# Retention and a SwiGLU block on one core: gate multiplies placed later, bank reads issued before retention steps, a third place for chunks

## The chip, the cores and the metric

The kernel runs on one core of a Trainium2 chip. Its time is device time in microseconds (us), the median of several runs. TensorE (PE) does matmuls into eight banks of PSUM; VectorE (DVE), ScalarE (ACT) and GpSimd (POOL) work on data in SBUF, the first two also read the banks; SyncE (SP) issues most of the DMA transfers, in order, from one queue. Each engine executes its own instructions in the order in which the program issued them. "PEld" is the loading of weights into PE, which overlaps the matmuls.

## The reference

```
state = gamma * state + k_t v_t^T          (per batch and head, for each t of 768)
y_t   = q_t state / sqrt(64)               -> x (3072 x 512): batch, time | head, dim
out   = (silu(x w_gate) * (x w_val)) w_out (512 -> 1536 -> 512)
```

Four batches, eight heads of 64, float32 throughout.

## The kernel before

Time is cut in chunks of 128 (six for each batch), and the work in four segments: a segment holds three chunks of each of two batches, so six chunks in all. The retention part of a chunk consists of `scores` (q and k against each other, masked by VectorE), `mix` (the output, copied to `xT` by ScalarE) and `state` (the running state). `retention(s)` returns these as a list of small steps, 24 with the sums behind them, and they are woven into other work.

All large products are done by Strassen's method in Winograd's form: 2 x 2 blocks, seven products in place of eight, with sums of blocks before and after. For segment 0, `up` computes gate and value block by block while the weights arrive. From segment 1 on, `up2` uses two nested levels, so the weights come as 21 units of seven blocks (three groups of four feature blocks, seven products each), in a ring of six slots, `ring[0]` to `ring[5]`. Where a unit's sums have not been made yet, `load_unit` fetches four blocks of seven from `unit_b`, `sums_u` makes the other three on VectorE in three steps (the last one also issues the store to `unit_t`). Later the whole unit is read from `unit_t`. Half of the units are summed during `down` of segment 0, the others in `up2` of segment 1.

`up2(s, prepared, at_end)` writes down the order by hand: each of its 21 stages registers events with a time, counted in products (stage n begins at 7 n; its seven products stand at +0, +2, ... +12, so two stages interleave), and the events are issued sorted by time. A product goes into bank `x`, `wb` or `z`; the next product into the same bank adds to it, so it waits until the last result has been read (events at +0.5, +2.5, ... +12.5, by ScalarE's copy or VectorE's add). GpSimd adds the blocks on the diagonal that ScalarE has copied (`pool`, +2.6). For product 3 of a group (`p == 3`), VectorE then multiplies the finished half `h0` with the gate in `p1` (line 564), in two blocks; for product 4 it does the same for `h1` (line 567).

`down(s, u, step)`, for three row blocks u, is the last product: seven products of six steps of k each (line 607), after four sums `sum_h` on VectorE (line 596; for u = 0 they stand ahead of `down`, later ones inside). After each product its helper calls `step`, 21 times for a segment, and `step` issues retention steps of the next segment (`retain`) and then, in segment 0, loads and sums of units; in later segments loads of the first units for the next `up2`. The two first products, `first(0)` and `first(1)`, need no sums.

A chunk is four tiles (`kt`, `qt`, `vn`, `kn`, 256 KB each). Two places for chunks lie in `loadp`. Two chunks are loaded ahead: in segment 0 after `up`, otherwise at the end of `up2`, as `loadp` comes free. Each further chunk is loaded by `last(n)` when the chunk two before it is done. GpSimd multiplies `kn` and `qt` by decays (lines 320 and 323) as soon as they are there.

Of the kernel before, what the change touches and what calls it, by code (L numbers as in the profile page):

```python
# [41 lines left out]
def tile_retnet_swiglu(  # L42
# [72 lines left out]

    def places_of(n):

        return [loadp[:, ts(4 * (n % 2) + i, 512)] for i in range(4)]

    def seg_chunks(s):  # L120

# [26 lines left out]
                          in_=wt[f].rearrange("p a (k f) -> p a k f", k=KH))  # L148

    units = {}  # L150
    ring_turn = [0]

    def load_unit(n, whole):
        t = ring[ring_turn[0] % RING].rearrange("p (h a b) -> p h a b", h=2, a=7)
        ring_turn[0] += 1
        if whole:
            nc.sync.dma_start(out=t, in_=unit_t[n])
        else:
            nc.sync.dma_start(out=t[:, :, ds(U11, 4)],
                              in_=unit_b[n // 7][:, SLOT[PRODUCTS[n % 7]]])  # L160
        units[n] = t
# [202 lines left out]
    def retention(s):  # L364

        cs = seg_chunks(s)

        def last(n):  # L370
            state(cs[n])
            del chunks[cs[n]]
            if s and n + 2 < len(cs):
                load_chunk(cs[n + 2], places_of(n))

        steps = [lambda: scores(cs[0])]
        for n, c in enumerate(cs):
# [106 lines left out]
    def up2(s, prepared, at_end):  # L484
# [23 lines left out]
        def stage(n):  # L508
            q, i = divmod(n, 7)
            base, odd, p = 7 * n, n % 2, PRODUCTS[i]  # L510
            halves = lambda b: banks[b][:, :TH].rearrange("p (h t) -> p h t", h=2)
            x = halves(((4, 0), (5, 1))[odd][n // 2 % 2])
            wb, z = halves(2 + odd), halves(6 + odd)
            h0, h1 = (hT[:, ds(4 * q, 4), i] for i in range(2))
            old, c = {1: (None, p1), 5: (None, p5), 6: (p1, u2), 2: (p1, p1),
                      7: (u2, u2), 3: (h0, h0), 4: (u2, u2)}[p]
            t = hsp[:, ds((2 + odd) * 4 * HT, 4 * HT)].rearrange(
                "p (m h t) -> p m h t", m=2, h=2)
            a = x1[p].rearrange("p k (h t) -> p k h t", h=2)
            sums = op2[p].rearrange("p (m t) -> p m t", m=4)  # L520

            def product(o, slot, rhs, start):
                w = units[n]
                for h in range(2):
                    nc.tensor.matmul(o[:, h], w[:, h, slot], rhs,  # L525
                                     start=(start and h == 0), stop=True,
                                     skip_group_check=True)
# [24 lines left out]

            def by_block(t1, t0, fn):

                for b, when in ((1, t1), (0, t0)):
                    at(base + when, fn, ds(2 * b, 2))

            if p in (6, 7):
                to = h0 if p == 6 else h1
                by_block(9.5, 13.5, lambda r: pool(to[:, r], u2[:, r], p5[:, r], op=add))  # L560
            elif p == 2:
                by_block(10.2, 14.2, lambda r: silu(p1[:, r]))
            elif p == 3:
                by_block(10.7, 13.7, lambda r: tt(h0[:, r], h0[:, r], p1[:, r], op=mul))  # L564
# [18 lines left out]
    def a_dn(i, j, u):  # L583
        return hT[:, ds(FH * j, FH), i, ts(u, P)]
# [11 lines left out]
        nc.vector.tensor_tensor(t, a, b, op=op)  # L596
        hs[n] = t

    first_dn = {}

    def down(s, u, step):
        x = banks[u % 2][:, :DH]
        cur = dict(hs)

        def product(o, slot, a, start=True):
            for k in range(FH):
                nc.tensor.matmul(o, a[:, k], wot[k][:, slot], start=(start and k == 0),  # L607
                                 stop=(k == FH - 1), skip_group_check=True)
            step()

        def tmp(i):
            return iop[:, ts(8 + i, DH)]

        def first(u):
            o = banks[u % 2][:, :DH]
            product(o, B11, a_dn(0, 0, u))
            first_dn[u] = tmp(u % 2)
            nc.scalar.copy(first_dn[u], o)

        def more(*ns):  # L620
            for n in ns:
                if u + 1 < L:
                    sum_h(n, u + 1)

        ev = [iop[:, ts(2 * (u % 2) + i, DM)] for i in range(2)]
        tt = nc.vector.tensor_tensor
        if u not in first_dn:
            first(u)
        if u == 0:
            first(1)  # L630
        p1 = first_dn.pop(u)
        wb = bank("wz")[:, :DH]
        product(wb, T1, cur[1])
        p5 = tmp(2)
        nc.scalar.copy(p5, wb)
        product(x, T2, cur[2], start=False)
        u2 = tmp(3)
        nc.scalar.copy(u2, x)
        product(wb, B22, cur[4], start=False)
        tt(ev[0][:, DH:], wb, u2, op=ALU.add)  # L640
        more(1, 2, 4)
        product(x, T3, cur[3], start=False)
        tt(ev[1][:, DH:], x, p5, op=ALU.add)  # L643
        more(3)
        z = bank("wz")[:, :DH]
        product(z, B21, a_dn(0, 1, u))
        tt(ev[0][:, :DH], z, p1, op=ALU.add)
        product(x, T4, a_dn(1, 1, u), start=False)
        nc.scalar.copy(ev[1][:, :DH], x)
        p, pos = divmod(s * L, NCK)  # L650
        for i in range(2):
            row = (2 * p + i) * S + (pos + u) * P
            nc.scalar.dma_start(out=out[ds(row, P)], in_=ev[i])


    def table(nm):
# [67 lines left out]
        late.pop(0)()  # L724


    resident = list(range(RING))
    to_sum = list(range(RING + 1, NU, 2)) + resident
    prepared = set(to_sum)

    for s in range(NSEG):
        nxt = seg_chunks(s + 1) if s + 1 < NSEG else []
        if s == 0:
            for i in range(2):
                load_chunk(nxt[i], places_of(i))
            ring_turn[0] = 4
        else:

            up2(s, prepared, [(7 * (NU - 5 + 2 * i) + 13.4,
                               lambda i=i: load_chunk(nxt[i], places_of(i)))  # L740
                              for i in range(2)] if nxt else [])
            prepared = set(range(NU))
        for n in (1, 2, 4, 3):
            sum_h(n, 0)
# [6 lines left out]
        def step():  # L751

            k = count[0] = count[0] + 1
            retain(1 + (k % 2 and 2 < k < 14))
            if not nxt:
                return
            if s:
                if k > 7 and k % 2 == 0 and k // 2 - 4 < RING:
                    load_unit(k // 2 - 4, True)
                return  # L760
            if count[1] < len(to_sum) and count[1] * 20 < (k + 2) * len(to_sum):
                load_unit(to_sum[count[1]], False)
                sums.extend(sums_u(to_sum[count[1]]))
                count[1] += 1
            while sums and count[2] * 20 < (k - 1) * 3 * len(to_sum):
                sums.pop(0)()
# [58 lines left out]
```

## Time and profile before

| | us |
|---|---|
| median of 3 runs | 788.09 |
| lowest and highest run | 785.54, 789.98 |
| the profiled execution's own time | 788.89 |
| its span, first to last instruction | 786.8 |
| first product of `down` in segment 0 | at 172.82 |
| `up2` of segments 1, 2, 3: first product to first product of `down` | 101.4, 101.9, 101.9 |
| `down` of segments 0, 1, 2: first product to first product of `up2` | 87.5, 79.5, 83.4 |

A line of the timeline gives the start, how long it lasts, the engine, the line of the program, the operation with its tiles and shapes and, in square brackets, how long the engine had been idle and what released it. A line of the waits gives the waiting engine and line, who released it, the us in total, the number of times and the longest one. A line of a window gives the busy time of PE, PEld, DVE, ACT and POOL in it, the clock granted to PE (1.00 is full speed), the share of the DMA engines that was busy and the GB/s. A product of `up2` is four matmul records (x4), one of `down` twelve.

### The profile page before, as it was taken

To read this page: it belongs to the slowest core of one execution; us is meant where nothing else is said; L and a number is where in the kernel's file an instruction comes from. 1 tells how busy PE (TensorE), PEld (TensorE's weight loads), DVE (VectorE), ACT (ScalarE), POOL (GpSimd) and SP (SyncE) were. 2 spreads that over 40 slices of the span, in tenths; PEclk is the share of its full clock that TensorE was granted. 3 is DMA by queue.
4 is the path that set the end of the run, shared out by engine and by line. 5 is a ranking of instruction groups with operands and counts; after the bars stand their busy time and mean duration, and the time that the engine had idled before them with its cause. 6 is when DMAs were issued, how large, how long until landed. Compare 5 with 4: busy or idle time off the path is not lost.

```text
span 786.8 us, 10948 instructions
## 1 busy us (share of the span) xinstructions
PE 731.1 (93%) x4196; PEld 630.0 (80%) x4196; DVE 493.5 (63%) x782; ACT 224.7 (29%) x440; POOL 288.9 (37%) x183
## 2 busy tenths in 40 slices
PE   5788889889799999999999999998999999998998
PEld 4655445558688989997888999997788899998886
DVE  2788888885758487877445366658265357567520
ACT  2464445411111324331212223331121133332100
POOL 3666666723110173554220072546120043727000
PEclk9999999999999999999999999999999999999999
DMA  9966676454789466752364255551157145640010
GB/s 318 304 194 213 210 246 212 164 186 173 269 293 360 162 207 233 258 204 89 104 241 178 74 189 186 188 174 41 61 174 281 47 150 187 215 152 1 1 53 28
DMA packets 60675, 138.08 MB, mean 175 GB/s; under 512 B 4560, under 2 KB 27600, under 8 KB 60624
## 3 DMA queue, kind: packets, MB, share of 16 engines
q1 hardware_dynamic: 57168, 131.09, 48.6%
q10 hardware_dynamic: 3456, 6.29, 2.3%
q8 instruction: 33, 0.54, 0.3%
q14 instruction: 18, 0.15, 0.1%
HBM read 100.80 MB, written 36.57 MB: 175 GB/s over the span
## 4 chain that ended last, share of the span: by engine, by line
PE 62%; DVE 11%; issue 3%; ACT 1%; DMA 1%; POOL 0%; ACTq 0%; SPq 0%; DVEq 0%
PE bank L525 30%; PE bank L607 23%; DVE hsp L596 3%; PE bank L359 2%; PE bank L308 2%; PE bank L355 2%; DVE iop L490 2%; PE bank L337 1%; PE bank L413 1%; DVE hT L564 1%; DMA loadp<-in_q_t_dram 1%; DVE hT L490 1%; DVE midp L314 1%; ACT midp L490 1%; DVE ring L169 1%
## 5 line engine op out<-in xcount | busy, mean ns | idle before, releaser
L525 PE MATMUL bank<-loadp,ring 128*128 128x192 f32 x720 | 141.0, 327 | 2.2 <-ACT midp L490 2.2
L607 PE MATMUL bank<-wot,hsp 128*128 128x256 f32 x576 | 132.2, 385 | 0.0
L525 PEld LDWEIGHTS bank<-loadp,ring 128*128 128x128 f32 x720 | 120.4, 190 | 4.9 <-ACT midp L490 4.9
L607 PEld LDWEIGHTS bank<-wot,hsp 128*128 128x128 f32 x576 | 108.7, 192 | 15.9 <-issue 0.7
L490 DVE TENSOR_TENSOR iop<-bank,iop 128x384 f32<-128x384 f32 x144 | 79.4, 553 | 61.3 <-PE bank L525 59.3
L607 PE MATMUL bank<-wot,hT 128*128 128x256 f32 x432 | 98.7, 382 | 2.7 <-DVE iop L643 2.7
L607 PEld LDWEIGHTS bank<-wot,hT 128*128 128x128 f32 x432 | 80.9, 190 | 15.3 <-DVE iop L643 3.2
L525 PE MATMUL bank<-xs,ring 128*128 128x192 f32 x432 | 87.9, 326 | 0.0
L490 POOL TENSOR_TENSOR iop<-hsp,midp 128x768 f32<-128x768 f32 x9 | 16.3, 1812 | 193.5 <-ACT hsp L490 193.5
L560 POOL TENSOR_TENSOR hT<-iop 128x768 f32<-128x768 f32 x36 | 66.5, 1847 | 35.8 <-DVE iop L490 35.8
L525 PEld LDWEIGHTS bank<-xs,ring 128*128 128x128 f32 x432 | 73.2, 190 | 0.0
L490 ACT COPY hsp<-bank 128x384 f32<-128x384 f32 x90 | 42.9, 479 | 99.5 <-PE bank L525 88.8
L525 PE MATMUL bank<-xT,ring 128*128 128x192 f32 x324 | 66.2, 327 | 2.3 <-DVE iop L490 2.3
L413 PE MATMUL bank<-xT,ring 128*128 128x384 f32 x144 | 54.6, 526 | 13.5 <-DVE hT L436 13.5
L413 PE MATMUL bank<-xs,ring 128*128 128x384 f32 x192 | 64.8, 488 | 1.8 <-DVE xs L397 1.0
L525 PE MATMUL bank<-hsp,ring 128*128 128x192 f32 x288 | 58.2, 330 | 8.1 <-DVE iop L490 8.1
L413 PEld LDWEIGHTS bank<-xs,ring 128*128 128x128 f32 x192 | 36.3, 191 | 28.9 <-ACT iop L432 1.9
L413 PEld LDWEIGHTS bank<-xT,ring 128*128 128x128 f32 x144 | 29.0, 205 | 36.2 <-issue 20.1
L525 PEld LDWEIGHTS bank<-xT,ring 128*128 128x128 f32 x324 | 54.8, 190 | 3.4 <-DVE iop L490 3.2
L525 PEld LDWEIGHTS bank<-hsp,ring 128*128 128x128 f32 x288 | 47.9, 190 | 11.2 <-DVE iop L490 10.5
L490 DVE TENSOR_TENSOR midp<-bank,midp 128x384 f32<-128x384 f32 x72 | 40.0, 555 | 26.1 <-PE bank L525 24.5
L362 ACT COPY xT<-bank 128x512 f32<-128x512 f32 x24 | 14.1, 587 | 146.8 <-PE bank L359 146.8
(120 smaller groups left out, 985.3 us busy)
## 6 DMA issues: line engine op xcount, KB each, us to landing
ring<-unitt SPq DMA_DIRECT2D x49, 896.0 KB, 4.6
unitt<-ring SPq DMA_DIRECT2D x21, 896.0 KB, 4.6
unitb<-ring SPq DMA_DIRECT2D x12, 896.0 KB, 4.9
ring<-unitb SPq DMA_DIRECT2D x21, 512.0 KB, 6.1
out_dram<-iop ACTq DMA_DIRECT2D x24, 256.0 KB, 2.3
loadp<-in_w_out_dram SPq DMA_DIRECT2D x20, 256.0 KB, 4.3
loadp<-in_k_t_dram SPq DMA_DIRECT2D x18, 256.0 KB, 4.8
loadp<-in_q_t_dram SPq DMA_DIRECT2D x18, 256.0 KB, 4.6
```

What stands on the lines that cost most here:

```text
L169: sub(w[:, :, U1 : U3 + 1 : 3], w[:, :, ds(U3, 2)], w[:, :, U11 : U3 + 1 : 2], op=ALU.subtract)
L308: nc.tensor.matmul(sp[i][:, ts(n, P)], kt[r, n], qt[r, n], start=True, stop=True, skip_group_check=True)
L314: nc.vector.tensor_tensor(t, pairs(sp[i]), mask[:, i], op=ALU.mult)
L355: nc.tensor.matmul(y[:, ts(n, P)], prev[:, n], qd[:, n], start=(n == 0), stop=False, skip_group_check=True)
L359: nc.tensor.matmul(y[ds(D * i, D), ts(n, P)], vn[:, ts(2 * n + i, D)], a[i][:, n], start=(ci == 0 and n == 0), stop=True, skip_group_check ...
L362: nc.scalar.copy(xT[:, :, c // NCK % 2, ts(ci % L, P)], pairs(y))
L413: nc.tensor.matmul(o, w[:, slot, k], a[:, k], start=(start and k == 0), stop=(stop and k == KH - 1), skip_group_check=True)
L490: events.append((t, len(events), lambda: fn(*args, **kw)))
L525: nc.tensor.matmul(o[:, h], w[:, h, slot], rhs, start=(start and h == 0), stop=True, skip_group_check=True)
L560: by_block(9.5, 13.5, lambda r: pool(to[:, r], u2[:, r], p5[:, r], op=add))
L596: nc.vector.tensor_tensor(t, a, b, op=op)
L607: nc.tensor.matmul(o, a[:, k], wot[k][:, slot], start=(start and k == 0), stop=(k == FH - 1), skip_group_check=True)
```

## The change

Four things. (1) The two multiplies of product 3's gate move from +10.7 and +13.7 to +15.8 and +14.3 (and change places). (2) In `down`, `step()` is called after the bank read that follows a product, not inside `product`; `retain` issues nothing at the first two calls, one retention step at the third and fourth, two at the fifth to twelfth, then one. (3) A third place for chunks lies in `ring[4]` and `ring[5]`. Three chunks are loaded ahead, and a further one when the chunk three before it is done. So during `down` the units use only four ring slots: twelve units instead of thirteen are summed in segment 0 (units 5, 7, ... 19 and 0 to 3), one more in `up2` of segment 1 (unit 4), and units 4 and 5 are loaded at the head of `up2`. (4) Two of the six steps of `first(0)` are issued inside the last stage of `up2`, ahead of its last product (`begin`).

```diff
     def places_of(n):
-        return [loadp[:, ts(4 * (n % 2) + i, 512)] for i in range(4)]
+        if n % 3 == 2:
+            return [ring[4 + i // 3][:, ts(i % 3, 512)] for i in range(4)]
+        return [loadp[:, ts(4 * (n % 3) + i, 512)] for i in range(4)]
...
-    def load_unit(n, whole):
-        t = ring[ring_turn[0] % RING].rearrange("p (h a b) -> p h a b", h=2, a=7)
-        ring_turn[0] += 1
+    def load_unit(n, whole, slot=None):
+        t = ring[n % RING if slot is None else slot]
+        t = t.rearrange("p (h a b) -> p h a b", h=2, a=7)
...
-            if s and n + 2 < len(cs):
-                load_chunk(cs[n + 2], places_of(n))
+            if s and n + 3 < len(cs):
+                load_chunk(cs[n + 3], places_of(n))
...
             elif p == 3:
-                by_block(10.7, 13.7, lambda r: tt(h0[:, r], h0[:, r], p1[:, r], op=mul))
+                by_block(15.8, 14.3, lambda r: tt(h0[:, r], h0[:, r], p1[:, r], op=mul))
...
     def down(s, u, step):
...
         def product(o, slot, a, start=True):
             for k in range(FH):
                 nc.tensor.matmul(o, a[:, k], wot[k][:, slot], start=(start and k == 0),
                                  stop=(k == FH - 1), skip_group_check=True)
-            step()
...
-        def first(u):
+        def first(u, ks=range(FH)):
             o = banks[u % 2][:, :DH]
-            product(o, B11, a_dn(0, 0, u))
-            first_dn[u] = tmp(u % 2)
-            nc.scalar.copy(first_dn[u], o)
+            for k in ks:
+                nc.tensor.matmul(o, a_dn(0, 0, u)[:, k], wot[k][:, B11], start=(k == 0),
+                                 stop=(k == FH - 1), skip_group_check=True)
+            if FH - 1 in ks:
+                first_dn[u] = tmp(u % 2)
+                nc.scalar.copy(first_dn[u], o)
+                step()
...
+        if u is None:
+            return first
...
-        if u not in first_dn:
+        if u == 0:
+            first(0, range(begun[0], FH))
+            first(1)
+        elif u not in first_dn:
             first(u)
-        if u == 0:
-            first(1)
...
         nc.scalar.copy(p5, wb)
+        step()
         product(x, T2, cur[2], start=False)
...
-    resident = list(range(RING))
-    to_sum = list(range(RING + 1, NU, 2)) + resident
+    resident = list(range(RING - 2))
+    to_sum = list(range(RING - 1, NU, 2)) + resident
...
-            for i in range(2):
+            for i in range(3):
                 load_chunk(nxt[i], places_of(i))
...
+            ends = [(7 * n + 13.4, lambda i=i: load_chunk(nxt[i], places_of(i)))
+                    for i, n in ((0, NU - 5), (2, NU - 4), (1, NU - 3)) if nxt]
+            def begin(s=s):
+                begun[0] = 2
+                down(s, None, None)(0, range(2))
+            ends.append((7 * (NU - 1) + 11, begin))
+            for n in range(RING - 2, RING):
+                ends.append((-1, lambda n=n: load_unit(n, n in prepared)))
+            up2(s, prepared, ends)
...
-            retain(1 + (k % 2 and 2 < k < 14))
+            retain((k > 2) + (4 < k < 13))
...
-                if k > 7 and k % 2 == 0 and k // 2 - 4 < RING:
+                if k > 7 and k % 2 == 0 and k // 2 - 4 < RING - 2:
                     load_unit(k // 2 - 4, True)
...
-                load_unit(to_sum[count[1]], False)
-                sums.extend(sums_u(to_sum[count[1]]))
+                n = to_sum[count[1]]
+                load_unit(n, False, n if n in resident else count[1] % (RING - 2))
+                sums.extend(sums_u(n))
```

More of the change, by code (lines that the diff above doesn't have):

```diff
@@ L150, in tile_retnet_swiglu @@
     units = {}
-    ring_turn = [0]
-    def load_unit(n, whole):
-        t = ring[ring_turn[0] % RING].rearrange("p (h a b) -> p h a b", h=2, a=7)
-        ring_turn[0] += 1
+    def load_unit(n, whole, slot=None):
+        t = ring[n % RING if slot is None else slot]
+        t = t.rearrange("p (h a b) -> p h a b", h=2, a=7)
         if whole:
@@ L597, in sum_h @@
         hs[n] = t
-    first_dn = {}
+    first_dn, begun = {}, [0]
     def down(s, u, step):
-        x = banks[u % 2][:, :DH]
+        x = banks[(u or 0) % 2][:, :DH]
         cur = dict(hs)
@@ L638, in down @@
         nc.scalar.copy(u2, x)
+        step()
         product(wb, B22, cur[4], start=False)
@@ L641, in down @@
         more(1, 2, 4)
+        step()
         product(x, T3, cur[3], start=False)
@@ L644, in down @@
         more(3)
+        step()
         z = bank("wz")[:, :DH]
@@ L647, in down @@
         tt(ev[0][:, :DH], z, p1, op=ALU.add)
+        step()
         product(x, T4, a_dn(1, 1, u), start=False)
@@ L653, in down @@
             nc.scalar.dma_start(out=out[ds(row, P)], in_=ev[i])
+        step()
     def table(nm):
@@ L733, in tile_retnet_swiglu @@
         if s == 0:
-            for i in range(2):
+            for i in range(3):
                 load_chunk(nxt[i], places_of(i))
-            ring_turn[0] = 4
         else:
-            up2(s, prepared, [(7 * (NU - 5 + 2 * i) + 13.4,
-                               lambda i=i: load_chunk(nxt[i], places_of(i)))
-                              for i in range(2)] if nxt else [])
+            ends = [(7 * n + 13.4, lambda i=i: load_chunk(nxt[i], places_of(i)))
[7 more added lines that the diff above has]
+            up2(s, prepared, ends)
             prepared = set(range(NU))
```

## The prediction

> **What bounds the kernel now.** I read the profile's page first, then the waits of TensorE (PE), then its timeline stage by stage.
>
> ```profile
> span 786.8 us, 10948 instructions
> ...
> PE 731.1 (93%) x4196; PEld 630.0 (80%) x4196; DVE 493.5 (63%) x782; ACT 224.7 (29%) x440; POOL 288.9 (37%) x183
> ```
>
> PE is busy for 731.1 of 786.8 us, so this kernel is a chain of matmuls with holes, and the most that a reordering can win is the 55.7 us of holes. Part of them lies in the load phase and in the first feed-forward pass, which the change doesn't touch. I therefore look for holes where it does: in the three `up2` passes and the four `down` passes. I write up2(1) for `up2` of segment 1, and so on.
>
> ```profile
> PE bank L525 <- DVE iop L490: 10.4, 10, 1.5
> ...
> PE bank L525 <- ACT midp L490: 2.2, 9, 0.5
> ```
>
> The columns are us in total, times, longest. In `up2` (line 525) PE waits 12.6 us in 19 places, always for a bank to be read. One of these places, in up2(2), the whole timeline around it, PE's matmuls with the other engines between:
>
> ```profile
> 468.97 0.81 PE L525 MATMUL bank<-xs,ring 128*128 128x192 f32 x4
> ...
> 469.82 0.56 DVE L490 TENSOR_TENSOR hT<-bank,hT 128x384 f32<-128x384 f32 x1 [0.67 <-PE bank L525]
> ...
> 470.11 1.81 POOL L490 TENSOR_TENSOR iop<-hsp,iop 128x768 f32<-128x768 f32 x1
> 470.29 2.45 DVE L564 TENSOR_TENSOR hT<-hT,midp 128x768 f32<-128x768 f32 x1
> ...
> 471.57 0.81 PE L525 MATMUL bank<-xT,ring 128*128 128x192 f32 x4
> ...
> 473.26 0.92 PE L525 MATMUL bank<-hsp,ring 128*128 128x192 f32 x4 [0.88 <-DVE iop L490]
> ...
> 474.06 0.94 DVE L564 TENSOR_TENSOR hT<-hT,midp 128x768 f32<-128x768 f32 x1
> ...
> 475.64 0.92 PE L525 MATMUL bank<-loadp,ring 128*128 128x192 f32 x4 [0.16 <-ACT midp L490]
> ```
>
> Here is the heart of the case. At 470.11 GpSimd starts a sum that lasts 1.81 us. At 470.29 VectorE starts a gate multiply of line 564 on data in SBUF; it takes 2.45 us, ending 0.8 us after GpSimd's sum, while the same multiply at 474.06, with GpSimd silent, takes 0.94 us. Everything behind it on VectorE is late, among it the read of a bank that PE needs at 472.22 and gets at 473.26. The multiply at 474.06 then delays ScalarE's copy into `midp`, and PE waits again until 475.64. From 468.97 to 471.57 lie four products, 0.65 us each; from 468.97 to 475.64 there should be eight, 5.20 us, and there are 6.67. One boundary between two groups of four blocks thus costs 1.47 us.
>
> **The change part by part: the gate multiplies.** The events of `up2` are sorted by time in products. The two multiplies go from 10.7 and 13.7 to 15.8 and 14.3: both behind the bank reads at 11.5, 12.5 and 13.5, one also behind that at 15.5. Nothing is added or removed. I work it through at the place above. A bank is read 0.85 us after its product's start (468.97, then 469.82) for about 0.55 us. The reads at 11.5, 12.5, 13.5 then start at 470.47, 471.12 and 471.77, the last ends at 472.33, and GpSimd ended at 471.92. So the first multiply runs free, 472.33 to 473.27. ScalarE's copy, which has to wait for it, ends at 473.8 if it takes as long as a bank read; PE needs it at 468.97 + 8 x 0.65 = 474.17. The read at 15.5 follows until 473.8, the second multiply until 474.8, the copy behind it until 475.3; PE needs that at 475.47. Both waits go, with margins of 0.4 and 0.2 us. I take the two boundaries of up2(2) and the two of up2(3) as alike: 2.9 us for each pass.
>
> At the end of a pass no next group overlaps, and the hole is larger. In up2(3):
>
> ```profile
> 723.06 0.81 PE L525 MATMUL bank<-hsp,ring 128*128 128x192 f32 x4
> ...
> 727.66 0.92 PE L525 MATMUL bank<-xT,ring 128*128 128x192 f32 x4 [0.69 <-DVE iop L490]
> 728.42 5.34 PE L607 MATMUL bank<-wot,hT 128*128 128x256 f32 x24
> 733.60 10.52 PE L607 MATMUL bank<-wot,hsp 128*128 128x256 f32 x48
> ```
>
> Four products remain from 723.06 on, so the pass should end at 725.66; `down` begins at 728.42, 2.76 us late. After the change the read of the product of 723.06 runs from 723.91 to 724.45, the first multiply to 725.4, the read at 15.5 to 725.95, and the last product can start at 726.0. PE would be there at 725.01; `begin` now puts two of the six steps of the first `down` product ahead of it. A product of `down` takes (733.60 - 728.42) / 2 = 2.59 us, two steps of it 0.86, so PE arrives at 725.87 and waits 0.15 us. Gain 2.6 us. In up2(2) GpSimd isn't silent there:
>
> ```profile
> 537.77 0.81 PE L525 MATMUL bank<-hsp,ring 128*128 128x192 f32 x4
> ...
> 538.73 1.76 POOL L320 TENSOR_TENSOR loadp<-loadp,tab 128x512 f32<-128x512 f32 x1
> ...
> 543.13 2.75 PE L607 MATMUL bank<-wot,hT 128*128 128x256 f32 x12
> ...
> 549.60 1.79 DVE L596 TENSOR_TENSOR hsp<-hT 128x768 f32<-128x768 f32 x1
> ...
> 552.05 1.75 PE L308 MATMUL bank<-loadp 64*128 64x128 f32 x16 [2.29 <-DVE midp L314]
> ...
> 553.73 4.54 PE L607 MATMUL bank<-wot,hsp 128*128 128x256 f32 x12
> ```
>
> The pass is again 2.76 us late (537.77 + 2.60 against 543.13). The moved multiply becomes due at 537.77 + 0.85 + 0.55 = 539.17, and GpSimd holds its multiply for the next segment's chunk from 538.73 to 540.49. Going by the 2.45 us row, VectorE waits for it, ends at 541.4, and the last product starts at 542.0 instead of 540.58. The gain is 1.3 us; it is 2.6 if the multiply gets in first, and I take the lower, since the row above shows the later one waiting.
>
> up2(1) is a case of its own, because VectorE also makes the weight units' sums there:
>
> ```profile
> PE bank L525 <- DVE iop L490: 2.5, 2, 1.5
> PE bank L525 <- ACT midp L490: 1.2, 3, 0.5
> ```
> ```profile
> L169 DVE TENSOR_TENSOR ring<-ring 128x512 f32<-128x512 f32 x21 | 17.4, 829 | 0.1
> ```
>
> Its waits are 3.7 us. Of them between -0.5 and 3.7 us can go: three unit sums (the largest 0.83 us) stay ahead of the moved multiplies at its first boundary, two chunk multiplies of GpSimd stand at its end, and unit 4 is now summed here too (three more instructions). I take 1.2 us, near the lower end, as both obstacles stay.
>
> **The order within `down`.** `step` is called behind the bank reads instead of ahead of them, and retention begins at the third call, not the first; by the tenth call both versions have issued 14 retention steps, so nothing is late at the end. The rows of 549.60 to 553.73 above show what it removes: the first scores' mask multiplies stand on VectorE behind four sums of `sum_h` (the last 1.79 us), and PE waits 2.29 us for them. Between 543.13 and 553.73 lie two products and two groups of scores.
>
> ```profile
> 172.82 2.75 PE L607 MATMUL bank<-wot,hT 128*128 128x256 f32 x12
> ...
> 181.42 2.86 PE L607 MATMUL bank<-wot,hsp 128*128 128x256 f32 x12
> ...
> 204.05 1.09 PE L359 MATMUL bank<-midp,loadp 128*64 128x128 f32 x16
> 207.54 2.86 PE L607 MATMUL bank<-wot,hT 128*128 128x256 f32 x12 [2.39 <-DVE iop L643]
> ...
> 217.92 1.16 PE L308 MATMUL bank<-loadp 64*128 64x128 f32 x16 [4.04 <-DMA loadp<-in_q_t_dram]
> 219.01 1.85 PE L355 MATMUL bank<-loadp,state 128*128 128x128 f32 x8
> 220.79 1.98 PE L359 MATMUL bank<-midp,loadp 128*64 128x128 f32 x16
> ```
> ```profile
> 361.68 2.75 PE L607 MATMUL bank<-wot,hT 128*128 128x256 f32 x12
> ...
> 370.48 2.86 PE L607 MATMUL bank<-wot,hsp 128*128 128x256 f32 x12
> ```
>
> A group of scores occupies 219.01 - 217.92 = 1.09 us, so two of each need 7.36 us. They took 8.60 in down(0), 8.80 in down(1), 10.60 in down(2). I leave 0.2 us in each for the changes of shape, and win 1.0, 1.2 and 3.0 us. Now the two first products run together, 4.32 us after the two steps already begun, and cover `sum_h` 1. At the end of up2(2) VectorE has, from 541.95 on, four operations of 0.94 us (a multiply of line 564, two of line 567, the first sum) and two reads of 0.55 ahead of T1: until 546.8. PE gets to T1 at 542.0 + 0.65 + 4.32 = 547.0. So 0.2 us of cover remain, and where they are gone T1 is late by as much as VectorE is.
>
> ```profile
> 220.00:222.50 2.50, 2.50 (x21) 2.14 (x19) 1.37 (x3) 0.00 (x0) 0.49 (x1) 0.50 0.79 305
> 553.80:556.00 2.20, 2.20 (x6) 1.76 (x7) 1.12 (x2) 0.00 (x0) 1.27 (x1) 0.50 0.00 0
> ```
>
> These rows (the third number from the end is the granted clock, here 0.50) price what follows a hole: in down(2) the next product took 4.54 us against 2.86 at 370.48, 1.7 us more, and in down(0) two groups ran at half clock for 3.83 us, 1.6 us more than they should. [...]
>
> In down(0), PE also waits 2.39 us at 207.54 for a bank read that stands behind a step's sums on VectorE; with the read issued first this goes.
>
> **The third place.** A chunk's four loads now follow the chunk three before it, not two.
>
> ```profile
> 211.28 0.84 SPq L112 DMA_DIRECT2D loadp<-in_q_t_dram  x1
> ```
> ```profile
> 260.29 0.81 PE L525 MATMUL bank<-xT,ring 128*128 128x192 f32 x4
> ```
> ```profile
> unitt<-ring SPq DMA_DIRECT2D x13, 896.0 KB, 4.7
> ring<-unitb SPq DMA_DIRECT2D x11, 512.0 KB, 6.4
> ```
>
> In down(0) the load of `q` was issued at 211.28, behind unit stores on SP's queue, which wait for VectorE's sums, and PE waited for it until 217.92, 4.04 us and then 1.6 us of slow clock. With three places this load is issued one chunk, two to three calls of `step`, earlier. The price: SP's queue in down(0) now cycles units through four ring slots instead of six. A reload has to wait for the store of the slot's last unit, and behind it on SP wait further stores and chunk loads. A call of `step` comes every 3.8 us (87.5 us from 172.82 to 260.29, less the 8.2 below, over 21 calls). The plan leaves 2 to 3 calls for a store that lands in 4.7 us, and 3 for a load that lands in 6.4 us, so I take it as covered and leave 0.8 us; bounds 0 and 5.6, the whole gain of this part. Units 4 and 5 are loaded at the head of `up2`, 28 products (18 us) before PE wants unit 4.
>
> The sum, against the profiled execution's own 788.9 us: down(0) 1.0 + 2.4 + 4.0 + 1.6 - 0.8 = 8.2; up2(1) 1.2; down(1) 1.2; up2(2) 2.9 + 1.3 = 4.2; down(2) 3.0 + 1.7 = 4.7; up2(3) 2.9 + 2.6 = 5.5; together 25.0. That gives 763.9. The profiled execution is 0.8 us above the median of the runs, less than their spread, so 764 us stands for the median too.
>
> **The rivals.** First, the chunk load stays late: SP serves its queue in order, and a wait for a store replaces the wait for a chunk. For it speaks that SP was the one late at 211.28, against it the lead of two to three calls. It keeps 5.6 us: 769.5. Second, the multiplies stay in PE's way: margins of 0.4 and 0.2 us are thin, and ScalarE's copies now wait for multiplies that come later. All four boundaries come back (5.8 us) and 0.8 of the ends: 770.6. Both together: 776. Third, nearly nothing is won: both of these, and T1 waits for `sum_h` in place of the scores, so that the 1.2 and 4.7 us of down(1) and down(2) come back too: 782, and with the odd new hole within 0.5% of before.
>
> Fourth, slower: the four slots make the unit traffic of down(0) a serial round. One unit is load, three sums and store, at most 6.4 + 2.5 + 4.7 = 13.6 us; twelve one after the other are 163 us, where down(0) has 87.5. The other stages win 16.8 us, so the kernel gets slower once down(0) exceeds 104.3 us, that is, with fewer than 1.56 units in flight; with 1.5 it ends at 793. Against it: four slots and loads three steps ahead of the sums allow two to three in flight, and a slot's turn of 6.7 calls is 25 us for a round of 13.6.
>
> **How the numbers follow.** Forecast 0.62; chunk load stays late 0.15; multiplies stay in the way 0.12; nearly nothing won 0.07, of which half within 0.5% (about what a measurement can tell from no change here); slower 0.04. So faster 0.92, same 0.04, slower 0.04. The range: all unknowns at their good ends (0.8 in down(0), 2.5 in up2(1), 1.3 in up2(2)) give 759, less 2 us for the spread of runs 757; at the other end both first rivals, 776.
>
> **What would show it.** Right: one multiply of line 564 takes about 1 us in the mean, PE's waits at line 525 fall from 12.6 to under 5 us, no wait for a chunk's `q` in down(0), two products stand together at the head of each `down`, and no half clock in down(2). Wrong: SP's queue waits for unit stores and VectorE for unit loads in down(0); ScalarE's `midp` copies still release PE; T1 waits for line 596. If down(0) stays above 85 us, my reading of the third place is wrong; if the up2 passes stay above 100 us, that of the multiplies.

## The result, and the profile after

The changed kernel takes 760.93 us (median of 4 runs, 760.26 to 762.35), the kernel before 789.04 in the same comparison; the ratio is 0.9649, 95% interval 0.9607 to 0.9691. The forecast was 764 us, range 757 to 776. The profiled execution took 760.26 us by its own time.

The page of the changed kernel, and its waits of PE:

```profile
span 758.5 us, 10969 instructions
...
PE 721.0 (95%) x4196; PEld 626.4 (83%) x4196; DVE 485.3 (64%) x782; ACT 225.4 (30%) x440; POOL 284.0 (37%) x183
```
```profile
PE bank L527 <- ACT midp L492: 2.8, 4, 1.3
...
PE bank L527 <- DVE iop L492: 1.1, 2, 0.7
```

PE's waits in `up2` fell from 12.6 us in 19 places to 3.9 in 6. No wait for line 607's or its successors' banks is left, nor one for a chunk in `down`. The place in up2(2) that the prediction works through, now (the line numbers have moved: 492 was 490, 527 was 525, 566 was 564):

```profile
456.76 0.81 PE L527 MATMUL bank<-xs,ring 128*128 128x192 f32 x4
...
457.90 1.81 POOL L492 TENSOR_TENSOR iop<-hsp,iop 128x768 f32<-128x768 f32 x1
...
459.62 0.56 DVE L492 TENSOR_TENSOR iop<-bank,iop 128x384 f32<-128x384 f32 x1
...
460.09 0.95 DVE L566 TENSOR_TENSOR hT<-hT,midp 128x768 f32<-128x768 f32 x1
...
461.15 0.48 ACT L492 COPY midp<-bank 128x384 f32<-128x384 f32 x1 [3.71 <-DVE hT L566]
...
461.96 0.81 PE L527 MATMUL bank<-loadp,ring 128*128 128x192 f32 x4
```

Eight products from 456.76 take until 461.96, that is 5.20 us: none is late. The multiply at 460.09 comes behind the bank read at 459.62, GpSimd's sum has ended at 459.71, and it lasts 0.95 us. ScalarE's copy at 461.15 waits for it and is in time.

PE's timeline gives each stage as the distance between its first product and that of the next stage. Two of the six steps of a `down` product (0.86 us) lie inside `up2` after the change, so 0.86 us of each `up2` belong to the `down` behind it (three steps, 1.29 us, in `best`; none in `no_begin` and the kernels whose names begin with `only`). down(3) goes to the end of the span. The last column adds all stages from the first product of `down` in segment 0 on, where the shift doesn't count.

| us | down(0) | up2(1) | down(1) | up2(2) | down(2) | up2(3) | down(3) | sum |
|---|---|---|---|---|---|---|---|---|
| before | 87.5 | 101.4 | 79.5 | 101.9 | 83.4 | 101.9 | 58.4 | 614.0 |
| after | 78.4 | 100.9 | 77.4 | 97.5 | 77.5 | 97.0 | 57.5 | 586.1 |
| `gates_back` | 78.4 | 102.5 | 77.5 | 102.0 | 77.5 | 101.9 | 57.5 | 597.1 |
| `step_first` | 78.8 | 100.1 | 77.4 | 97.5 | 77.5 | 97.0 | 57.5 | 585.8 |
| `retain_early` | 79.3 | 100.9 | 81.8 | 97.5 | 83.9 | 97.0 | 57.4 | 597.9 |
| `two_places` | 83.5 | 100.9 | 79.3 | 97.5 | 81.5 | 97.1 | 57.5 | 597.4 |
| `no_begin` | 78.4 | 100.9 | 78.2 | 97.5 | 78.4 | 97.0 | 58.4 | 588.7 |
| `only_gates` | 88.3 | 100.1 | 80.1 | 97.5 | 81.9 | 97.0 | 58.4 | 603.4 |
| `only_place` | 80.3 | 101.4 | 80.2 | 101.9 | 82.9 | 101.9 | 58.4 | 607.1 |
| `only_order` | 83.6 | 102.1 | 80.2 | 100.7 | 82.2 | 101.9 | 58.4 | 609.0 |
| `best` | 78.4 | 98.6 | 77.4 | 97.3 | 77.2 | 97.0 | 57.1 | 582.8 |

The sum is the better measure for single parts: the load phase and the first feed-forward pass, which none of these kernels changes, ended anywhere from 172.4 to 175.8 us, and this moves the medians by up to 3 us.

### The profile page after: what moved, and what is told of

Same layout as the page of the kernel before. It is cut to its first block, busy times and chain, and to the rows that moved or that the text cites. A ratio compares the mean times of both kernels' runs of the same rounds, so it can differ in the third digit from the quotient of the medians.

```text
span 758.5 us, 10969 instructions
## 1 busy us (share of the span) xinstructions
PE 721.0 (95%) x4196; PEld 626.4 (83%) x4196; DVE 485.3 (64%) x782; ACT 225.4 (30%) x440; POOL 284.0 (37%) x183
## 4 chain that ended last, share of the span: by engine, by line
PE 75%; DVE 2%; issue 1%; ACT 0%; ACTq 0%; DVEq 0%
PE bank L527 37%; PE bank L611 24%; PE bank L620 4%; PE bank L310 3%; PE bank L361 2%; PE bank L357 2%; PE bank L339 2%; PE bank L415 1%; DVE iop L492 0%; DVE hsp L482 0%; ACT midp L492 0%; DVE hsp L481 0%; DVE hsp L484 0%; DVE hsp L483 0%; ACTq L668 0%
## 5 line engine op out<-in xcount | busy, mean ns | idle before, releaser
L611 PEld LDWEIGHTS bank<-wot,hsp 128*128 128x128 f32 x576 | 107.8, 190 | 15.8 <-issue 0.5
L611 PE MATMUL bank<-wot,hT 128*128 128x256 f32 x288 | 65.9, 382 | 0.0
L611 PEld LDWEIGHTS bank<-wot,hT 128*128 128x128 f32 x288 | 53.8, 190 | 8.1 <-issue 1.4
L364 ACT COPY xT<-bank 128x512 f32<-128x512 f32 x24 | 14.1, 586 | 100.7 <-PE bank L361 100.7
```

The lines of the kernel that those rows point to most:

```text
L364: nc.scalar.copy(xT[:, :, c // NCK % 2, ts(ci % L, P)], pairs(y))
```

## The experiments

Five kernels undo one part each of the changed kernel, one puts a part of it in another order, three make one part alone in the kernel before, one takes GpSimd's sum out of that kernel, and one goes on from the changed kernel.

**Multiplies back (`gates_back`).**

```diff
-                by_block(15.8, 14.3, lambda r: tt(h0[:, r], h0[:, r], p1[:, r], op=mul))
+                by_block(10.7, 13.7, lambda r: tt(h0[:, r], h0[:, r], p1[:, r], op=mul))
```

> The changed kernel (760.9 us) with the gate multiplies back at +10.7 and +13.7. Theory (they queue behind GpSimd's sums and ahead of the bank reads): the four boundaries of up2(2) and up2(3) lose 1.47 us each again, 5.9 us; the three ends of a pass lose 0.5 to 1.5 us each, as the two steps of the first down product still cover part; up2(1) about 1: in all 768 to 771 us, with single multiplies of over 2 us. Rival (the gain came from the order in down, and the multiplies hide in any place): under 764 us.

Measured: 773.05 us, ratio to before 0.9807 (0.9763 to 0.9851); the sum is 11.0 us longer, all of it in `up2`. The same place of up2(2):

```profile
460.78 1.81 POOL L492 TENSOR_TENSOR iop<-hsp,iop 128x768 f32<-128x768 f32 x1
...
460.96 2.45 DVE L566 TENSOR_TENSOR hT<-hT,midp 128x768 f32<-128x768 f32 x1
...
463.93 0.92 PE L527 MATMUL bank<-hsp,ring 128*128 128x192 f32 x4 [0.88 <-DVE iop L492]
...
466.31 0.92 PE L527 MATMUL bank<-loadp,ring 128*128 128x192 f32 x4 [0.16 <-ACT midp L492]
```

The multiply starts behind GpSimd's sum again and takes 2.45 us, and both waits are back. At the three ends the cover of the two product steps remains, but up2(2) and up2(3) still lose over a microsecond there each (a wait of 1.53 us). The theory holds. The time is above the 768 to 771 us expected; 1.2 us of the profiled run's difference lie ahead of `down`, in a part that the edit doesn't touch.

**GpSimd's sum left out (`no_pool_sum`, on the kernel before).**

```diff
-                at(base + 2.6, pool, diagonal(c), t, diagonal(old), op=add)
+                if p != 4:
+                    at(base + 2.6, pool, diagonal(c), t, diagonal(old), op=add)
```

> The kernel before without GpSimd's sum of product 4 (its diagonal blocks are left out), multiplies at their old places. Theory (a multiply takes 2.45 us since GpSimd's sum holds what it needs): all multiplies of line 564 near 0.95 us, the holes of 1.47 us at the four boundaries shrink below 0.5 us, 779 to 782 us. Rival (the multiplies cost through their place in the queue alone): the boundaries stay at 1 us or more, 785 us or more.

Measured: 775.9 us (one run); up2(2) and up2(3) take 98.1 and 97.4 us. The multiplies stand where they always stood:

```profile
466.28 0.81 PE L525 MATMUL bank<-xs,ring 128*128 128x192 f32 x4
...
467.61 0.95 DVE L565 TENSOR_TENSOR hT<-hT,midp 128x768 f32<-128x768 f32 x1
...
471.48 0.90 PE L525 MATMUL bank<-loadp,ring 128*128 128x192 f32 x4
```

From 466.28 to 471.48 are 5.20 us for eight products. With GpSimd silent the multiply takes 0.95 us, not 2.45, and the old place costs nothing at this boundary. So it was not the place among the bank reads by itself, it was the overlap with GpSimd. The run is faster than the 779 to 782 us expected: 3 us come from a shorter wait for a chunk in down(0), 0.9 instead of 4.0 us, and 1.7 us from down(2), where the product behind a hole of 2.35 us took 2.86 us, not 4.54; this edit aims at neither.

**Multiplies alone (`only_gates`).** The diff of `gates_back` the other way, in the kernel before.

> The kernel before with the gate multiplies alone at +15.8 and +14.3. Theory: boundaries 5.9 us, up2(1) 1 to 2, ends about 1.5 each of the three without the covering product steps: 776 to 779 us. Rival (the holes in up2 are filled, but the multiplies then stand later in VectorE's queue and delay the sums ahead of the first scores, so the holes in down grow): 782 to 786 us.

Measured: 779.64 us, ratio 0.9864 (0.982 to 0.9909), sum 10.6 us shorter. `up2` gains its full 10.6 us. The time is just above what was expected (776 to 779 us), and under the rival's 782 to 786. The rival's mechanism is there too, though small:

```profile
550.53 1.76 PE L308 MATMUL bank<-loadp 64*128 64x128 f32 x16 [2.52 <-DVE midp L314]
552.21 2.86 PE L607 MATMUL bank<-wot,hsp 128*128 128x256 f32 x12
```
```profile
552.50:555.00 2.50, 2.50 (x13) 2.19 (x13) 0.90 (x2) 0.00 (x0) 1.14 (x1) 1.00 0.00 0
```

The wait ahead of the second scores grew from 2.29 to 2.52 us in down(2), and in down(1) from 0.49 to 1.11, since the multiplies now stand nearer to the sums. What hides it is the luck of the clock: behind the 2.52 us it stayed at 1.00 (third number from the end), and the next product took 2.86 us, not 4.54.

**Multiplies exchanged (`gates_swapped`).**

```diff
-                by_block(15.8, 14.3, lambda r: tt(h0[:, r], h0[:, r], p1[:, r], op=mul))
+                by_block(14.3, 15.8, lambda r: tt(h0[:, r], h0[:, r], p1[:, r], op=mul))
```

> The changed kernel with the two multiplies in the other order, block 1 at +14.3 and block 0 at +15.8. Theory (ScalarE's first copy of the next group overwrites block 0 of the gate, so it waits for that multiply): the copy ends about 1.5 us later, against a margin of 0.4 us, about 1 us at each of six boundaries, 766 to 768 us. Rival (ScalarE has slack, and only the distance to GpSimd's sums counts): 761 us.

Measured: 761.94 us, 0.9641 (0.9626 to 0.9655): no difference. The expectation overlooked what the edit does. The copy of the next group is issued at +14.5, so block 0's multiply at +15.8 comes behind it in program order and uses the next group's values; it is the multiply that waits for the copy, not the other way round. This run changes the computation in that block and says nothing on the margin. The order of the events tells why the multiplies changed places: block 0 has to come ahead of +14.5, block 1 ahead of +16.5.

**Retention from the first call (`retain_early`).**

```diff
-            retain((k > 2) + (4 < k < 13))
+            retain(1 + (k % 2 and 2 < k < 14))
```

> The changed kernel with retention begun at the first call of step again; the reads stay ahead of it. Theory (the masks behind the four sums of down make PE wait, and the clock falls to half behind the hole of over 2 us in down(2)): 1.0 + 1.2 + 4.7 = 6.9 us back, 767 to 769 us, with a clock of 0.50 behind a hole of about 2.3 us. [...] Second rival (the sums are no longer in the way, since the multiplies of up2 end earlier): under 763 us.

Measured: 772.98 us, 0.9808 (0.9772 to 0.9844); 11.8 us longer, nearly twice the 6.9 expected. In down(1) and in down(2):

```profile
361.10 1.75 PE L310 MATMUL bank<-loadp 64*128 64x128 f32 x16 [1.97 <-DVE midp L316]
362.78 4.54 PE L611 MATMUL bank<-wot,hsp 128*128 128x256 f32 x12
```
```profile
536.61 1.90 DVE L598 TENSOR_TENSOR hsp<-hsp,hT 128x768 f32<-128x768 f32 x1
...
541.75 2.67 PE L310 MATMUL bank<-loadp 64*128 64x128 f32 x16 [3.26 <-DVE midp L316]
...
544.35 4.44 PE L611 MATMUL bank<-wot,hsp 128*128 128x256 f32 x12
```
```profile
363.00:365.50 2.50, 2.50 (x8) 1.96 (x8) 0.97 (x2) 0.00 (x0) 0.00 (x0) 0.55 0.00 0
544.00:546.00 2.00, 2.00 (x6) 1.51 (x6) 1.29 (x2) 0.00 (x0) 1.50 (x2) 0.50 0.00 0
```

The holes that were 0.49 and 2.29 us in the kernel before are 1.97 and 3.26 us here. With the moved multiplies alone (`only_gates`) they were 1.11 and 2.52 us, since VectorE comes later; PE also arrives 0.86 us earlier (the begun steps), and that makes 1.97 and 3.38, near what is measured. Behind both holes the clock is at about half (0.55 and 0.50 in the windows above), and a product takes 4.54 and 4.44 us, as the theory has it. The rival by which the sums are no longer in the way fails, since they are in the way more than before. The late start of retention is thus the part that makes the other two safe.

**Step ahead of the reads (`step_first`).** `step()` goes back into `product`, ahead of the bank read; retention still begins at the third call.

```diff
         def product(o, slot, a, start=True):
             for k in range(FH):
...
+            step()
...
-        step()
         product(x, T2, cur[2], start=False)
...
```

> The changed kernel with step called inside each product again, ahead of the bank read; the later start of retention is kept. Theory (the hole of 2.39 us in down(0) came from the read behind a step's sums on VectorE): down(0) longer by 2 to 3 us, the other down stages by under 1 us each: 763 to 765 us. Rival (the three places and the later start removed that hole as well): 761 us, no hole in down(0).

Measured: 762.67 us, 0.9673 (0.9639 to 0.9708); the sum is not longer. PE waits 0.18 us in down(0) for the read that had cost 2.39:

```profile
202.63 2.86 PE L611 MATMUL bank<-wot,hT 128*128 128x256 f32 x12 [0.18 <-DVE iop L654]
```

The rival is right: with the other parts in place, issuing the reads first is worth 0.4 us in down(0). The run's median is 1.7 us longer because its down(0) begins at 174.27, 1.9 us later than in the changed kernel; up2(1) is 0.8 us shorter, by a hole at its head that comes up again under `best`.

**Two places (`two_places`).** All other parts stay; chunks have two places, units six ring slots.

```diff
-        if n % 3 == 2:
-            return [ring[4 + i // 3][:, ts(i % 3, 512)] for i in range(4)]
-        return [loadp[:, ts(4 * (n % 3) + i, 512)] for i in range(4)]
+        return [loadp[:, ts(4 * (n % 2) + i, 512)] for i in range(4)]
...
-                load_chunk(cs[n + 3], places_of(n))
+                load_chunk(cs[n + 2], places_of(n))
...
-    resident = list(range(RING - 2))
-    to_sum = list(range(RING - 1, NU, 2)) + resident
+    resident = list(range(RING))
+    to_sum = list(range(RING + 1, NU, 2)) + resident
...
```

> The changed kernel with two places for chunks, six ring slots for units, thirteen units summed in segment 0 again. Theory (the third place took away the wait for q in down(0) and the half clock behind it): 5.6 us back, 766 to 767 us, with a wait of some 4 us for a chunk. Rival (that wait came from VectorE's late unit sums ahead of it in SP's queue, and the new order in down makes these earlier): under 763 us and no wait for a chunk.

Measured: 773.34 us, 0.9803 (0.9759 to 0.9846), 11.2 us longer: 5.1 in down(0), 1.9 in down(1), 4.0 in down(2). PE waits for a chunk's `q` in all three; here SP's queue and PE in down(2):

```profile
PE bank L311 <- DMA loadp<-in_q_t_dram: 7.2, 3, 3.0
```
```profile
568.49 0.33 SPq L112 DMA_DIRECT2D loadp<-in_q_t_dram  x1
```
```profile
575.42 1.60 PE L311 MATMUL bank<-loadp 64*128 64x128 f32 x16 [2.30 <-DMA loadp<-in_q_t_dram]
576.95 4.05 PE L612 MATMUL bank<-wot,hsp 128*128 128x256 f32 x12
```

In down(0) the theory's 5.6 us come back nearly as forecast. The waits in down(1) and down(2) (575.42 is 6.9 us after the issue at 568.49) are new: neither kernel has them, and the 766 to 767 us expected had no place for them. Retention that begins later and then runs two steps a call wants its chunks sooner than two places let them come.

**Third place alone, order alone (`only_place`, `only_order`).** The kernel before with the third place and its ring slots, and with the new order in `down` (reads first, late retention), each without the other parts.

> The kernel before with the third place alone (four ring slots for units in down, order of steps and multiplies as before). Theory (it removes the wait for q in down(0) and the half clock behind it, nothing in the other stages): down(0) 81 to 83 us instead of 87.5, the hole of 2.4 us at line 643's read stays, other stages within 0.7 us: 783 to 785 us where before has 788. Rival (chunk loads still stand behind unit stores that now wait for ring slots): down(0) 86 us or more, 787 us or more.

> The kernel before with the new order in down alone (reads ahead of step, retention begun at the third call, two per call later), two places for chunks, multiplies at their old places, no product steps in up2. Theory (the later and denser retention needs its chunks sooner than two places can give them, as with two_places): waits for q of 2 to 3 us in all three down stages, so down(0) about 83.5, down(1) 79.5, down(2) 81.5: a gain of 5 to 6 us. Rival (the waits for q came from the multiplies and the begun product; the order alone keeps its worth): down(1) 78.3, down(2) 78.5, a gain of 9 us or more.

Measured: 784.02 us, 0.9938 (0.9911 to 0.9966), sum 6.9 us shorter; and 784.1 us, 0.9931 (0.9902 to 0.996), 5.0 us shorter. The third place takes down(0) from 87.5 to 80.3 us: no wait for a chunk, and the hole at the bank read shrinks as well, from 2.39 us to

```profile
209.03 2.86 PE L611 MATMUL bank<-wot,hT 128*128 128x256 f32 x12 [0.95 <-DVE iop L654]
```

without any change in the order of reads. The expectation had this hole stay; why it shrinks is open. `only_order` has the three waits for `q` of `two_places` again (7.2 us together), so its gain in down(0) stops at 3.8 us and down(1) is 0.7 us longer than before. Its rival fails: the waits don't come from the multiplies or the begun product.

Of the 5.0 us of `only_order`, 1.2 lie in up2(2), which the edit doesn't touch. At one boundary there the multiply (line 567 in this kernel), at its old place, started before GpSimd's sum:

```profile
502.01 0.95 DVE L567 TENSOR_TENSOR hT<-hT,midp 128x768 f32<-128x768 f32 x1
502.20 2.44 POOL L493 TENSOR_TENSOR iop<-hsp,iop 128x768 f32<-128x768 f32 x1
```

Now the multiply takes 0.95 us and the sum 2.44, and PE doesn't wait. In the kernel before, the sum of this boundary (503.54) starts 0.18 us ahead of the multiply; then the sum takes 1.81 us and the multiply 2.43. Of these two pairs the one that started second was held up, on either engine.

**No steps of `down` inside `up2` (`no_begin`).** The event of `begin` is left out.

> The changed kernel without the two steps of the first down product inside up2. Theory: the last product of each pass waits 0.86 us more for a bank read, less what the read is earlier than PE: 0.8 us for each of three passes, 763 to 764 us. Rival (PE finds the work right behind and nothing is lost): 761 us.

Measured: 765.0 us, 0.9679 (0.9663 to 0.9695); the sum is 2.6 us longer, 0.8 to 0.9 for each pass. At the end of up2(2):

```profile
529.09 0.54 DVE L492 TENSOR_TENSOR iop<-bank,iop 128x384 f32<-128x384 f32 x1
...
529.69 0.92 PE L527 MATMUL bank<-xT,ring 128*128 128x192 f32 x4 [1.24 <-DVE iop L492]
```

The last product waits 1.24 us for the bank read at 529.09; with the two steps ahead of it, it waited 0.38 us in the changed kernel. The 0.86 us between are the two steps: all of their time is hidden.

**Three more edits (`best`).** The changed kernel has two holes of over 1 us left, both in up2(1): 1.32 us at the first boundary, where VectorE makes the unit sums, and this one at the head:

```profile
250.93 0.37 ACT L664 COPY iop<-bank 128x256 f32<-128x256 f32 x1 [9.99 <-PE bank L611]
250.99 1.63 ACTq L668 DMA_DIRECT2D out_dram<-iop  x2
...
252.72 0.86 ACT L492 COPY midp<-bank 128x384 f32<-128x384 f32 x2 [1.42 <-DVE hsp L484]
...
253.25 0.92 PE L527 MATMUL bank<-loadp,ring 128*128 128x192 f32 x4 [1.06 <-ACT midp L492]
```

ScalarE issues two output transfers at 250.99, which takes 1.63 us, and its copy, for which PE waits 1.06 us, stands behind them. The profile puts the copy's wait down to VectorE's sum of line 484, which ends at the same moment. But where the issue took 0.85 us (the kernel before, at 260.55), PE waited 0.27 us (in `step_first` 0.28), and in `best`, where SyncE issues these transfers, the copy runs at 251.74, before that sum, at 252.44.

```diff
-            nc.scalar.dma_start(out=out[ds(row, P)], in_=ev[i])
+            dma = nc.sync if u == L - 1 and s < NSEG - 1 else nc.scalar
+            dma.dma_start(out=out[ds(row, P)], in_=ev[i])
...
-                for when, k in ((2.2, 0), (4.8, 1), (6.8, 2)):
+                for when, k in ((9.2, 0), (11, 1), (13.2, 2)) if n == 6 else (
+                        (2.2, 0), (4.8, 1), (6.8, 2)):
...
-                begun[0] = 2
-                down(s, None, None)(0, range(2))
+                begun[0] = 3
+                down(s, None, None)(0, range(3))
```

> The changed kernel with three more edits: the last output row blocks of a segment issued by SyncE instead of ScalarE (the hole of 1.06 us at the head of up2(1) is ScalarE issuing two output DMAs for 1.63 us ahead of its copy), unit 8's three sums moved behind the multiplies (hole of 1.32 us at the first boundary of up2(1)), three steps of the first down product instead of two ahead of the last product. Theory: up2(1) shorter by 2 to 3 us, the heads of up2(2) and up2(3) by 0.2, the ends by 0.4: 757 to 759 us where the changed kernel has 761. Rival (the holes are filled by the next wait in line, the sums ahead of the copy): 760 us or more.

Measured: 758.24 us (757.26 to 760.65), 0.9623 (0.9586 to 0.9659) against before; the sum is 3.3 us shorter than after, 2.3 of it in up2(1). After the first product of `down` in segment 0, two holes are left in the whole kernel, 0.27 and 0.23 us. The run doesn't tell the three edits apart; the two holes of up2(1) that it fills were 2.4 us. The intervals of this kernel and of the changed one overlap, so that the stages show the gain, not the ratios.

## Why the prediction was right

Stage by stage, with the 0.86 us counted where the prediction counted them: down(0) gained 9.1 us (forecast 8.2), up2(1) 1.4 (1.2), down(1) 1.3 (1.2), up2(2) 5.3 (4.2), down(2) 5.0 (4.7), up2(3) 5.8 (5.5): together 27.8 us for 25.0. down(0) is better by the 0.8 us left for the four ring slots, which cost nothing: PE is busy for all of its 78.37 us.

One premise was wrong. The 55.7 us of holes aren't the most that can be won: PE's idle time fell by 18.2 us, to 37.5, and its busy time by 10.1, to 721.0. A boundary that cost 1.47 us showed 0.88 and 0.16 us of idle time; the products beside a hole are drawn longer (0.92 us for 0.81), and those at half clock count as busy (4.54 us for 2.86 at 553.73).

**The multiplies.** Both halves of the argument are shown: the waits come back with the old places (`gates_back`) and go without GpSimd's sum (`no_pool_sum`), and one goes where the multiply starts first (`only_order`). The six multiplies of up2(2) and up2(3) that took 2.43 to 2.45 us are down to 0.95, except one of 1.45 at the end of up2(2). In the pairs shown, the one that started second was held up: the multiply of 470.29 started 0.18 us behind GpSimd's sum and ended 0.82 us after it, nearly its own 0.94, and in `only_order` GpSimd's sum started 0.19 us behind the multiply and took 2.44 us for 1.81.

**The end of up2(2)** was mis-sized: 1.3 us forecast, 2.1 measured. I took GpSimd's chunk multiply at the 1.76 us of the row of 538.73.

```profile
522.41 1.46 PE L527 MATMUL bank<-hsp,ring 128*128 128x192 f32 x8
...
523.38 1.04 POOL L322 TENSOR_TENSOR loadp<-loadp,tab 128x512 f32<-128x512 f32 x1
...
523.79 1.45 DVE L566 TENSOR_TENSOR hT<-hT,midp 128x768 f32<-128x768 f32 x1
524.36 1.03 PE L620 MATMUL bank<-wot,hT 128*128 128x256 f32 x4
...
525.76 0.92 PE L527 MATMUL bank<-xT,ring 128*128 128x192 f32 x4 [0.38 <-DVE iop L492]
...
526.52 4.48 PE L620 MATMUL bank<-wot,hT 128*128 128x256 f32 x20
```

Now it takes 1.04 us. The old row came behind a VectorE multiply, which the prediction doesn't show:

```profile
537.14 2.44 DVE L564 TENSOR_TENSOR hT<-hT,midp 128x768 f32<-128x768 f32 x1
```

That one ended at 539.58, so GpSimd's multiply of 538.73 ran beside it for 0.85 us; it ended 0.91 us after it and took 0.72 us more than now. The moved multiply now ends at 525.24, again 0.82 us after GpSimd, and PE waits 0.38 us, not 1.4. In that stretch both durations, 1.76 us on GpSimd and 2.44 on VectorE, hold more than the operation's own 1.04 and 0.94. The pass was 2.76 us late; now `down` goes on at 526.52, which is 0.65 us late if one takes off the 0.86 us begun and counts four products of 0.65 from the one that starts at 522.41.

**up2(1)** is right by two errors that cancel: the first boundary still waits 1.32 us, as the unit sums stay in front (moved in `best`, they cost nothing), and a new hole of 1.06 us stands at the head, which I hadn't thought of; the second boundary and the end gained more. That the sum came out is luck.

**The head of `down`.** Two products together cover `sum_h` 1 with little to spare, as forecast:

```profile
526.52 4.48 PE L620 MATMUL bank<-wot,hT 128*128 128x256 f32 x20
...
529.41 0.96 DVE L598 TENSOR_TENSOR hsp<-hT 128x768 f32<-128x768 f32 x1
...
530.83 2.75 PE L611 MATMUL bank<-wot,hsp 128*128 128x256 f32 x12
533.52 1.16 PE L310 MATMUL bank<-loadp 64*128 64x128 f32 x16
```

The sum ends at 530.37; T1 follows at 530.83 without a wait, and takes 2.75 us, not 4.54. But the prediction's 1.0, 1.2 and 3.0 us for the later retention, and 1.7 of clock, measure the part in the old surroundings; in the new ones leaving the late start out costs 11.8 us.

What I didn't see: the hole of 2.29 us in down(2) was for the most part the same clash of VectorE and GpSimd. Two views of the kernel before, down(2) and down(1):

```profile
547.77 1.91 DVE L596 TENSOR_TENSOR hsp<-hT,hsp 128x768 f32<-128x768 f32 x1
...
548.82 1.75 POOL L320 TENSOR_TENSOR loadp<-loadp,tab 128x512 f32<-128x512 f32 x1
```
```profile
366.32 0.96 DVE L596 TENSOR_TENSOR hsp<-hT,hsp 128x768 f32<-128x768 f32 x1
...
368.80 1.75 PE L308 MATMUL bank<-loadp 64*128 64x128 f32 x16 [0.49 <-DVE midp L314]
```

In down(2) GpSimd multiplies a chunk beside the last two sums, which take 1.91 and 1.79 us; in down(1) it is silent and they take 0.96 and 0.95. That is 1.79 us, and the holes, 2.29 and 0.49, differ by 1.80. In the changed kernel GpSimd starts there at 534.79, behind the sums, so the later retention moves this clash away as well.

**The third place.** The load of the fifth chunk's `q`, the one that was late, is now issued at 198.51, and its scores run at 209.93, 11.4 us later:

```profile
198.51 0.85 SPq L112 DMA_DIRECT2D loadp<-in_q_t_dram  x1
```
```profile
209.93 1.16 PE L310 MATMUL bank<-loadp 64*128 64x128 f32 x16
```

The forecast gave it 5.6 us in down(0), and `two_places` lost 5.1 there. What I didn't see is that the later, denser retention needs the third place in down(1) and down(2) as well, 5.9 us more. And the 2.39 us, which I put down to the reads alone, has two cures: the reads first, or the third place (0.95 us left with it alone). With all parts in place either does.

The parts interlock. Alone, multiplies, place and order win 10.6, 6.9 and 5.0 us (1.2 of the 5.0 in up2(2), as told above), and the begun steps, tried in the changed kernel only, are worth 2.6: 25.1 us of the 27.8. Taken out one by one, the multiplies, the place, the late start of retention and the begun steps cost 11.0, 11.2, 11.8 and 2.6 us, together far more than was won.

## What to carry to other kernels

When two engines slow each other, look for the operation that starts while the other engine's is running, and move it behind. Don't take its duration in that stretch for its cost. Price each part in the schedule that the other parts leave: one that lets work begin later asks for its data faster, and one that lets PE arrive earlier opens the next wait. Where the stages ahead of the change scatter by microseconds, compare the stages, not the totals.

## What the runs showed of the hardware

In `down`, the clock of PE fell to about half behind holes of 1.97 us (0.55 in the window shown), 2.29 and 2.30 us (0.50), and behind all of 3 us and more (0.50 behind 3.00, 3.26, 4.04 and 4.05, 0.53 behind 3.21), and stayed at 1.00 behind holes of 1.86, 1.96, 2.39 and 2.52 us. Behind others the next product of `down` tells: 4.54 us behind 2.02 (`only_order`) and 2.42 us (`no_pool_sum`), 3.62 behind 2.29 (`only_place`), 2.86 behind 2.35 (`no_pool_sum`) and 2.44 us (`only_gates`). Ahead of `down`, in the part that no edit touches, eight matmuls took 2.82 us behind a hole of 3.45 us (`only_place`, 141.36) and one of 3.46 (`step_first`, 139.88), but 4.51 us behind one of 3.46 in the changed kernel (139.49, with a clock of 0.50 in 140.00:142.00). So a hole of about 2 us cost 1.7 us more behind it (4.54 us for 2.86), or less, or nothing. What decides stays open.

The issue of two output transfers held ScalarE for 1.63 us in the changed kernel, while SP was issuing a load (251.16, 0.94 us), and for 0.85 us at the same place before (260.55), where SP issued none; whether that makes the difference wasn't tried.
